# A fused Fourier mixing and squared-ReLU FFN on Trainium2: a third PSUM buffer out of the transform's banks, and more steps with P-Q+N on VectorE

## The chip, the cores and the metric

The kernel runs on one core of one Trainium2 chip. A core has five engines with a queue of instructions each, executed in order and tied together by semaphores: TensorE (PE; its weight loads are shown as PEld), VectorE (DVE), ScalarE (ACT), GpSimd (POOL) and SyncE (SP, which here only issues DMAs). Matmuls write to PSUM, which has 8 banks of 512 float32 columns in each of 128 partitions; VectorE and ScalarE read it. The metric is the device time of one execution in microseconds.

## The reference

```python
X = np.fft.fft(x, axis=1)              # x: 8 x 3008 x 256
X = np.fft.fft(X, axis=2)
t = X.real.reshape(8 * 3008, 256)
h = np.maximum(t @ w_in, 0.0)          # w_in: 256 x 2048
return h * h @ w_out                   # w_out: 2048 x 256
```

For each of 8 batches the real part of a two-dimensional Fourier transform is taken, and every one of the 24064 rows then goes through a feed-forward layer with 2048 hidden values, a ReLU and a square.

## The kernel before

**Pairs of tokens.** The second transform (over 256 values) is folded into `w_in` at the start: `gh[:, 0]` and `gh[:, 1]` are the cosine and the sine part of it times `w_in`, `gh[:, 2]` is the sine part times -2. With `zc` and `zs`, the cosine and sine parts of the first transform at a frequency k, the hidden values before the ReLU are P+Q for token k and P-Q (with a correction N for one row) for its mirror token S-k. So only half of the frequencies are computed: 12040 columns, in 25 windows or blocks (`wins`): 240, 512, 376, 376, 512, 448, then 512 each, and 360 in the last, block 24. Block w makes the hidden values of its columns and their mirrors.

**A block's steps.** A block has 8 steps (the loop at L1001), each for 256 of the 2048 hidden values (two chunks of 128). There are two kinds:

- A plain step: `pq` (L864) makes P+Q with four matmuls in a PSUM tile `ph` of two banks; ACT takes the ReLU out of it (`relu`, L893, with sign 0); `turn` (L888) adds -2Q with two more matmuls, which makes P-Q in the same tile; ACT takes that ReLU too (sign 1). DVE then squares the whole of both halves (`power`, L905).
- A step in `diff[w]`: `cosines` (L873) makes P alone with two matmuls; DVE makes t = -2P+N from it (`twice`, L879, from the rows `n` that POOL makes); `sines` (L883) adds Q with two matmuls; ACT takes the ReLU of P+Q and squares it (`power_act`, L909); DVE makes the ReLU of P-Q+N by a saturating add of t and `ph` (L898) and squares that half. Such a step has no `turn`.

`ph` has two buffers (`ps_h`, four banks). The saturating add of a step in `diff` is put off (`pend`) until behind the next step's `twice` if that step is in `diff` too. Where two such steps stand before a step, the next plain step begins with one piece of the second matmul of the FFN (L1024) ahead of `pq`. Squares are put off (`kept`) until the next step's `settle`. Between `pq` or `cosines` and `turn` or `sines`, `others` (L918) issues the rest of the step's work: the folds of the next batch (DVE, and transfers on POOL's queue), a part of the second matmul `po` (L713) of the block before, from its `h2`, and matmuls of the next window's transform. Most steps have 16 matmuls of `po`, of 256 columns; ACT copies `po` out to `osb` (L728), and SP's queue stores that.

**The transform's matmuls.** `z_steps` makes a unit (a batch's odd or even frequencies): four parts in the order zs/first, zc/first, zs/second, zc/second (`part` 1 is the sine part). Each part is an accumulation over 3 matmuls (odd) or 4 or 6 (even) in a PSUM tile `pz` of one bank, from a pool `ps_z` of two (L541). When a first part ends, ACT copies it to `es` (L548). The second parts go on in the tile that `st[part]` then names, a new one only where h and k are 0; ACT copies their sums into `zc` or `zs` (L554), and DVE makes the other half of the frequencies out of `es` and the same sums (`minus`, `apart`, L572). While `held["on"]` is set, which is where the next step is in `diff`, `minus` is kept back until `settle` has run in that step or until a new part begins (`let_go`). The matmuls of a unit are spread evenly over the steps from `lo` to `hi` of the block before the one that needs them.

**Order.** The order on every engine is the order of the program's text; there is no scheduler (`manual_schedule`). The framework follows tiles: it sets the semaphore waits between engines from the tiles that instructions read and write.

The last block's output (`tail`, L697) takes a PSUM tile for each group of 128 tokens, groups 2 and 3 of four from `ps_z` (L707).

Of the kernel before, what the change touches and what calls it, by code (L numbers as in the profile page):

```python
# [16 lines left out]
P = 128  # L17
R = 6
# [11 lines left out]
def kernel(  # L30
# [80 lines left out]
    drp = ctx.enter_context(tc.tile_pool(name="drp", bufs=2, space=bass.MemoryType.DRAM))  # L111
    ps_h = ctx.enter_context(tc.tile_pool(name="ps_h", bufs=2, space=bass.MemoryType.PSUM))
    ps_o = ctx.enter_context(tc.tile_pool(name="ps_o", bufs=2, space=bass.MemoryType.PSUM))
    ps_z = ctx.enter_context(tc.tile_pool(name="ps_z", bufs=2, space=bass.MemoryType.PSUM))

    XW = R * D

# [214 lines left out]
    def fold_steps(i):  # L332
# [42 lines left out]
        def v_part(sg):  # L375
# [6 lines left out]
                nc.vector.tensor_copy(ev[:, :, 0, 0:1], w[:, :, 0:1])  # L382
            nc.gpsimd.memset(ev[:, :, sg, 129:130], 0.0)

        def d_even(h=None):
            a, z = (0, 4 * R) if h is None else (2 * R * h, 2 * R * (h + 1))
            if a == 0:
                for o, v in ((t[0:1, 2, 0, :], t[0:1, 0, R - 1, :]), (fef[:, :, 0:1], xf[:, :, 0:1])):
                    if i > 1:
                        nc.scalar.activation(o, v, AF.Copy, bias=0.0, scale=1.0)  # L390
                    else:
                        nc.vector.tensor_copy(o, v)
            nc.vector.tensor_tensor(fef[:, a:z, 1:129], lo[:, a:z], hi[:, a:z], op=ALU.add)

        def d_odd(h=None):
# [72 lines left out]
            cp(spn[:, :, :, 0:1], rev_dim(yt[:, :, 0, :, 128:129], 1))  # L468

        late = [lambda: fold8(0), lambda: fold8(1), lambda: fold16(0), lambda: fold16(1), nyq8]  # L470
        return {"u_row": u_row, "edge": edge, "u_half": u_half, "u_odd": u_odd, "u_part": u_part, "v_even": v_even, "v_part": v_part, "d_even": d_even, "n_cos": n_cos, "odds": odds, "d_odd": d_odd, "load": load, "n_sin": n_sin, "nyq": nyq, "even": even, "away": away, "back": back, "late": late}

    gh = const.tile([P, 3, F], F16, name="gh")

# [47 lines left out]
    def z_steps(u, late=False):  # L522
# [15 lines left out]
        def mm(part, h, k, last, o0, o1, lhs, tab):  # L538
            if h == 0 and k == 0:
                let_go()  # L540
                st[part] = ps_z.tile([P, 512], F32, name="pz", tag="pz")  # L541
            ps = st[part]
            nc.tensor.matmul(ps[:, o0:o1], lhs, tab, start=(h == 0 and k == 0), stop=last, skip_group_check=True)  # L543
            if not last:
                return
            if h == 0:
                es = st["es", part] = evp.tile([P, NE], F32, name="es", tag="es")
                nc.scalar.activation(es[:, 0:n], ps[:, 0:n], AF.Copy, bias=0.0, scale=1.0)  # L548
                return
            es = st["es", part]  # L550
            for w, o, a, cnt in spans(c0, n):
                if late and w > 0:
                    continue
                nc.scalar.activation(zwin(w)[part][:, o : o + cnt], ps[:, a : a + cnt], AF.Copy, bias=0.0, scale=1.0)  # L554
            if not late:
                minus(part)
# [45 lines left out]
    def run(*jobs):  # L602
        for j in jobs:
            j()
# [91 lines left out]
    def ffn2_steps(w, h2, tail=False):  # L696
# [6 lines left out]
        def part(i, hf):  # L703
            q, m = groups[i]
            j = 0 if tail else i % 2
            if tail and hf == 0 and i % 4 > 1:
                st["po", i] = ps_z.tile([P, 512], F32, name="po", tag="pz")  # L707
            elif j == 0 and hf == 0:
                st["po", i] = ps_o.tile([P, 512], F32, name="po", tag="po")
            po = st["po", i - j]  # L710
# [40 lines left out]
    NST = NFC // 2  # L751
    at_of = {w: [[] for _ in range(NST)] for w in range(NW)}
    post_of = {w: [[] for _ in range(NST)] for w in range(NW)}
    diff = {w: (4, 6) if w < 6 else (1, 3, 5, 7) if w < NW - 4 else (1, 2, 4, 6, 7) for w in range(3, NW)}
    backs = []
    shared = []

    def put(w, s, i, name, *k, d=at_of):
        d[w][s].append(lambda: folds[i][name](*k))
# [1 line left out]
    def late(w, s, i, *st):  # L761
        at_of[w][s].append(lambda: run(*[folds[i]["late"][k] for k in st]))
# [4 lines left out]
    for i in range(2, B):  # L767
        b0 = (win_of(col_of[i, 0]) + win_of(col_of[i - 1, 1])) // 2 - 1
        tight = b0 - 2 in [(win_of(col_of[j, 0]) + win_of(col_of[j - 1, 1])) // 2 - 1 for j in range(2, i)]
        near = i == 2 or tight  # L770
        at_of[b0 - 1][0].append(lambda i=i: make(i))
        at_of[b0 - 2][7].append(lambda i=i: load_rows(i))
        backs.append(b0)
        late(b0 + 1, 3, i, 0)
        late(b0 + 1, 4, i, 1)
        for k in (2, 3, 4):
            late(b0 + 1, 5, i, k)
        put(b0 - 1, 5 if near else 3, i, "d_even", 0)
# [24 lines left out]
    plus = []  # L803
    pend = []

    def settle():
        for k in kept:
# [22 lines left out]
    for w in range(NW):  # L830
# [40 lines left out]
        t2s = {}  # L871

        def cosines(s):  # L873
            ph = phs[s] = ps_h.tile([P, 2, 512], F32, name="ph", tag="psh")
            for a in range(2):
                f0 = (2 * s + a) * P
                nc.tensor.matmul(ph[:, a, 0:wn], gh[:, 0, f0 : f0 + P], zcw[:, 0:wn], start=True, stop=True)  # L877
# [123 lines left out]
        for s in range(NST) if w > 1 else ():  # L1001
            held["on"] = s + 1 in diff.get(w, ())
            if s in diff.get(w, ()):
# [27 lines left out]
            nyq(s)  # L1031
            turn(s)
            relu(s, 1)
            if w in shared and s == 5:
                power_act(4, 1)
            keep(s, int(s == NST - 1), 2)
# [35 lines left out]
```

## Time and profile before

| | |
|---|---|
| median of 3 runs | 596.65 us (596.57 to 596.75) |
| the profiled execution | 596.79 us |
| its span, first to last instruction | 595.0 us |
| TensorE busy | 586.2 us (99%), 4430 matmuls |
| VectorE busy | 499.4 us (84%) |
| ScalarE busy | 463.0 us (78%) |
| GpSimd busy | 242.2 us (41%) |
| mean granted TensorE clock | 0.999 |

The views used are the page (busy times; 40 slices of the span; groups of instructions by line and form, with count, busy time, mean length of one, and the idle time of the engine ahead of them with what ended it), the sums of busy time in chosen windows, and the timeline (start, length, engine, line, operation and tiles, count of merged instructions). Times in the timeline count from the span's start. A row with a count of 2 or more runs from the first one's start to the last one's end; a matmul's row is longer than the distance to the next matmul, because matmuls overlap. The blocks begin at: 3 at 70.36, 6 at 133.60, 9 at 204.34, 10 at 229.72, 11 at 254.21, 21 at 492.86, 22 at 515.18, 23 at 538.71, 24 at 561.04; the last block's steps end at 580.4.

### The profile page before, as it was taken

The numbers are of one execution on the slowest core, as the hardware profiler recorded it, in microseconds if no ns is written. First come the engines' busy times: TensorE is split into PE (matmuls) and PEld (weight loads), VectorE is DVE, ScalarE is ACT, GpSimd is POOL, SyncE is SP. The second block draws the span as 40 slices with busy tenths as digits, with TensorE's granted clock in tenths as the row PEclk, the third lists the DMA queues.
The fourth block names the chain that finished last, engine by engine and source line by source line (L and its number), as shares of the span: only waits on it lengthen the run. The fifth ranks groups of instructions, "written<-read, shape, count | busy, mean of one in ns | idle before, by whom it ended". The sixth has DMA issues, their size and how long they took to land.

```text
span 595.0 us, 11318 instructions
## 1 busy us (share of the span) xinstructions
PE 586.2 (99%) x4430; PEld 426.0 (72%) x4430; DVE 499.4 (84%) x584; ACT 463.0 (78%) x620; POOL 242.2 (41%) x301
## 2 busy tenths in 40 slices
PE   9899999999999999999999999999999999999997
PEld 4567786776776777777777777777777777777786
DVE  8988686987889788978899899978899999889871
ACT  6796877967787787788878788877877788788762
POOL 8320423266504606182254651546505624425310
PEclk9999999999999999999999999999999999999999
DMA  8945421237211551246113442145312311211212
GB/s 150 170 86 135 124 72 44 54 102 150 58 47 52 134 133 53 73 99 151 42 58 113 94 115 55 38 121 117 88 39 90 89 56 37 61 47 48 61 56 70
DMA packets 37624, 50.33 MB, mean 85 GB/s; under 512 B 4589, under 2 KB 30755, under 8 KB 37571
## 3 DMA queue, kind: packets, MB, share of 16 engines
q0 software_dynamic: 10400, 24.94, 20.5%
q1 hardware_dynamic: 26899, 24.44, 13.6%
q8 instruction: 34, 0.56, 0.4%
q10 hardware_dynamic: 272, 0.23, 0.1%
q14 instruction: 19, 0.16, 0.1%
HBM read 36.42 MB, written 27.86 MB: 108 GB/s over the span
## 4 chain that ended last, share of the span: by engine, by line
PE 85%; DVE 7%; ACT 5%; issue 2%; ACTq 0%; DVEq 0%
PE po L713 48%; PE ph L891 7%; PE ph L868 7%; PE ph L869 7%; PE ph L886 6%; PE ph L877 5%; PE pz L543 4%; DVE h L907 2%; ACT h L900 2%; PE pw L310 2%; DVE t L881 2%; DVE h L898 2%; ACT h L911 1%; PE pg L489 1%; DVE zc L572 1%
## 5 line engine op out<-in xcount | busy, mean ns | idle before, releaser
L713 PE MATMUL po<-wout,h 128*128 128x256 f16 (+1 forms) x3024 | 364.8, 273 | 0.0
L713 PEld LDWEIGHTS <-h 128*128 128x128 f16 (+1 forms) x3024 | 296.9, 98 | 75.1
L900 ACT ACTIVATE h<-ph 128x1024 f16<-128x1024 f32 (+3 forms) x301 | 287.6, 991 | 64.2 <-PE ph L886 39.7
L907 DVE TENSOR_TENSOR h<-h 128x2048 f16<-128x2048 f16 (+7 forms) x199 | 193.2, 977 | 21.9 <-ACT h L900 16.9
L827 POOL TENSOR_SCALAR n<-zn,g2n 128x512 f32<-128x512 f16 (+3 forms) x166 | 155.6, 951 | 68.7 <-DMA zn<-rd 51.6
L881 DVE SCALAR_TENSOR_TENSOR t<-ph,n 128x1024 f32<-128x1024 f32 (+3 forms) x83 | 99.1, 1194 | 35.3 <-PE ph L877 31.7
L898 DVE CUSTOM_DVE_ANT_0 h<-t,ph 128x1024 f16<-128x1024 f32 x74 | 90.0, 1217 | 15.1 <-ACT h L900 13.8
L911 ACT ACTIVATE h<-h 128x1024 f16<-128x1024 f16 (+3 forms) x87 | 90.4, 1039 | 0.5
L728 ACT ACTIVATE osb<-po 128x512 f32<-128x512 f32 (+3 forms) x95 | 55.1, 585 | 37.0 <-PE po L713 32.5
L868 PE MATMUL ph<-zc,gh 128*128 128x512 f16 (+3 forms) x218 | 80.3, 369 | 0.4 <-ACT h L959 0.3
L869 PE MATMUL ph<-zs,gh 128*128 128x512 f16 (+3 forms) x218 | 80.2, 368 | 0.0
L819 POOL DMA_DIRECT2D zn<-rd x22 | 12.9, 585 | 161.4 <-DMA rd<-zs 146.3
L891 PE MATMUL ph<-zs,gh 128*128 128x512 f16 (+3 forms) x218 | 62.5, 368 | 0.4 <-ACT h L900 0.4
L886 PE MATMUL ph<-zs,gh 128*128 128x512 f16 (+3 forms) x166 | 48.4, 373 | 0.9 <-DVE t L881 0.4
L877 PE MATMUL ph<-zc,gh 128*128 128x512 f16 (+3 forms) x166 | 48.4, 373 | 0.0
L868 PEld LDWEIGHTS <-gh 128*128 128x128 f16 x218 | 21.2, 97 | 22.9 <-DVE h L898 1.6
L869 PEld LDWEIGHTS <-gh 128*128 128x128 f16 x218 | 21.3, 98 | 22.1 <-issue 0.9
L877 PEld LDWEIGHTS <-gh 128*128 128x128 f16 x166 | 16.2, 98 | 19.0 <-issue 0.5
L891 PEld LDWEIGHTS <-gh 128*128 128x128 f16 x218 | 20.2, 98 | 4.1 <-issue 0.7
L426 POOL DMA_DIRECT2D scr<-ev x8 | 4.7, 593 | 42.1 <-DVE ev L422 36.4
L548 ACT ACTIVATE es<-pz 128x376 f32<-128x376 f32 (+1 forms) x32 | 14.8, 485 | 8.9 <-PE pz L543 8.9
L436 POOL DMA_INDIRECT rb<-scr,idx_r x16 | 18.7, 1167 | 4.9 <-issue 4.9
(144 smaller groups left out, 368.6 us busy)
## 6 DMA issues: line engine op xcount, KB each, us to landing
out_dram<-osb SPq DMA_DIRECT2D x77, 128.0 KB
xo<-in_x_dram POOLq DMA_DIRECT2D x7, 768.0 KB
scr<-ev POOLq DMA_DIRECT2D x8, 390.0 KB
zn<-rd POOLq DMA_DIRECT2D x19, 128.0 KB
rb<-scr POOLq DMA_DIRECT2D x16, 130.0 KB
out_dram<-osb SPq DMA_DIRECT2D x12, 94.0 KB
w<-in_moe_w_in_dram POOLq DMA_DIRECT2D x2, 512.0 KB
wout<-in_moe_w_out_dram POOLq DMA_DIRECT2D x1, 1024.0 KB
```

The lines of the kernel that those rows point to most:

```text
L713: nc.tensor.matmul(po[0:m, j * D : (j + 1) * D], h2[:, fc, q : q + m], wout16[:, fc, :], start=(fc == 0 and not both), stop=(fc == NFC - 1 ...
L827: nc.gpsimd.tensor_scalar(out=n2[:, a, 0:wn1], in0=zns[wt][:, 0:wn1], scalar1=g2n[:, fc : fc + 1], scalar2=1.0, op0=ALU.mult, op1=ALU.mult)
L868: nc.tensor.matmul(ph[:, a, 0:wn], gh[:, 0, f0 : f0 + P], zcw[:, 0:wn], start=True, stop=False)
L869: nc.tensor.matmul(ph[:, a, 0:wn], gh[:, 1, f0 : f0 + P], zsw[:, 0:wn], start=False, stop=True)
L877: nc.tensor.matmul(ph[:, a, 0:wn], gh[:, 0, f0 : f0 + P], zcw[:, 0:wn], start=True, stop=True)
L881: nc.vector.scalar_tensor_tensor(out=t2[:, :, 0:wn], in0=phs[s][:, :, 0:wn], scalar=-2.0, in1=n2s[w, s][:, :, 0:wn], op0=ALU.mult, op1=ALU ...
L886: nc.tensor.matmul(phs[s][:, a, 0:wn], gh[:, 1, f0 : f0 + P], zsw[:, 0:wn], start=False, stop=True, skip_group_check=True)
L891: nc.tensor.matmul(phs[s][:, a, 0:wn], gh[:, 2, f0 : f0 + P], zsw[:, 0:wn], start=False, stop=True, skip_group_check=True)
L898: nc.vector._custom_dve(TENSOR_ADD_SAT, out=h, in0=t2s[s][:, :, 0:wn], in1=phs[s][:, :, 0:wn], s0=BIG, s1=0.0)
L900: nc.scalar.activation(h, phs[s][:, :, 0:wn], AF.Relu, bias=0.0, scale=-1.0)
L907: nc.vector.tensor_tensor(h, h, h, op=ALU.mult)
L911: nc.scalar.activation(h, h, AF.Square, bias=0.0, scale=1.0)
```

## The change

- The pool of two one-bank tiles for the transform becomes a single two-bank tile `zz`. A transform's new part takes its first or second bank in turn. The last block's output groups 2 and 3 of four take its banks too.
- In blocks 21, 23 and 24 (`threes`), the tiles `ph` go round three buffers: the two of `ps_h` and `zz`. Blocks 21 and 23 have no transform to make; block 22 has.
- `diff` changes: block 6 from (1, 3, 5, 7) to (1, 2, 4, 6, 7); block 9 from (1, 3) to (1, 2, 4); blocks 21 and 23 from (1, 2, 4, 6, 7) to (1, 2, 3, 5, 6, 7); block 24 from (1, 2, 4, 6, 7) to (1, 2, 3, 4, 5, 6, 7). That makes 89 such steps instead of 83.
- In blocks 21 and 23 the squares of the halves P-Q+N are put off to the next plain step (`aside`, on DVE) or given to ACT (`aside_act`, steps 3 and 7); in block 24 ACT squares those of steps 2 and 5. Block 6 joins the blocks in which ACT squares that half of step 4 (`shared`).
- In those three blocks the piece of the second matmul ahead of `pq` is left out.
- The two row copies at the head of `d_even` become a function `d_rows`, put one step earlier in block 9. The load of the input of transform 3 (`i + 1 = 3`) moves from block 5, step 7, to block 6, step 2.

```diff
-    ps_z = ctx.enter_context(tc.tile_pool(name="ps_z", bufs=2, space=bass.MemoryType.PSUM))
+    ps_z = ctx.enter_context(tc.tile_pool(name="ps_z", bufs=1, space=bass.MemoryType.PSUM))
+    zz = ps_z.tile([P, 2, 512], F32, name="zz")
+    turn_of = {"z": 0, "ph": 0}
...
+        def d_rows():
+            for o, v in ((t[0:1, 2, 0, :], t[0:1, 0, R - 1, :]), (fef[:, :, 0:1], xf[:, :, 0:1])):
...
-                st[part] = ps_z.tile([P, 512], F32, name="pz", tag="pz")
+                st[part] = zz[:, turn_of["z"] % 2, :]
+                turn_of["z"] += 1
...
-                st["po", i] = ps_z.tile([P, 512], F32, name="po", tag="pz")
+                st["po", i] = zz[:, i % 2, :]
...
-    diff = {w: (4, 6) if w < 6 else (1, 3, 5, 7) if w < NW - 4 else (1, 2, 4, 6, 7) for w in range(3, NW)}
+    diff = {w: (4, 6) if w < 6 else (1, 3, 5, 7) if 6 < w < NW - 4 else (1, 2, 4, 6, 7) for w in range(3, NW)}
+    diff[NW - 4] = diff[NW - 2] = (1, 2, 3, 5, 6, 7)
+    diff[NW - 1] = (1, 2, 3, 4, 5, 6, 7)
+    threes = (NW - 4, NW - 2, NW - 1)
+    by_act = (2, 5)
     backs = []
-    shared = []
+    shared = [6]
...
+        put(b0 - 1, 4 if tight else 5 if near else 3, i, "d_rows")
...
-        if i + 1 < B and b0 > 5 and (win_of(col_of[i + 1, 0]) + win_of(col_of[i, 1])) // 2 - 1 > b0 + 2:
+        if i + 1 < B and (win_of(col_of[i + 1, 0]) + win_of(col_of[i, 1])) // 2 - 1 > b0 + 2:
             put(b0 + 1, 2, i, "load")
...
         if tight:
-            diff[b0 - 1] = (1, 3)
+            diff[b0 - 1] = (1, 2, 4)
...
+        def bank():
+            if w in threes:
+                turn_of["ph"] += 1
+                if turn_of["ph"] % 3 == 0:
+                    return zz
+            return ps_h.tile([P, 2, 512], F32, name="ph", tag="psh")
+
         def pq(s):
-            ph = phs[s] = ps_h.tile([P, 2, 512], F32, name="ph", tag="psh")
+            ph = phs[s] = bank()
...
-                whole = w in shared and s == 4
+                whole = w in shared and s == 4 or w in threes[:2] or w == NW - 1 and s in by_act
                 pend.append(lambda s=s, r=relu, k=keep, whole=whole: (r(s, 1), whole or k(s, 1, 2)))
+                if w in threes[:2] and s % 4 < 3:
+                    aside.append(lambda s=s, p=power: p(s, 1, 2))
...
+                act_squares()
+                if w in threes[:2] and s % 4 == 3 or w == NW - 1 and s in by_act:
+                    aside_act.append(lambda s=s, p=power_act: p(s, 1))
...
-            if made[s] and made[s + 1]:
+            if made[s] and made[s + 1] and w not in threes:
                 f2s[s].pop(0)()
             pq(s)
+            kept.extend(aside)
+            aside.clear()
             settle()
```

More of the change, by code (lines that the diff above doesn't have):

```diff
@@ L383, in v_part @@
             nc.gpsimd.memset(ev[:, :, sg, 129:130], 0.0)
+        def d_rows():
+            for o, v in ((t[0:1, 2, 0, :], t[0:1, 0, R - 1, :]), (fef[:, :, 0:1], xf[:, :, 0:1])):
+                if i > 1:
+                    nc.scalar.activation(o, v, AF.Copy, bias=0.0, scale=1.0)
+                else:
+                    nc.vector.tensor_copy(o, v)
         def d_even(h=None):
             a, z = (0, 4 * R) if h is None else (2 * R * h, 2 * R * (h + 1))
[L387 to L392, printed above, removed]
+            if h is None:
+                d_rows()
             nc.vector.tensor_tensor(fef[:, a:z, 1:129], lo[:, a:z], hi[:, a:z], op=ALU.add)
@@ L470, in fold_steps @@
         late = [lambda: fold8(0), lambda: fold8(1), lambda: fold16(0), lambda: fold16(1), nyq8]
-        return {"u_row": u_row, "edge": edge, "u_half": u_half, "u_odd": u_odd, "u_part": u_part, "v_even": v_even, "v_part": v_part, "d_even": d_even, "n_cos": n_cos, "odds": odds, "d_odd": d_odd, "load": load, "n_sin": n_sin, "nyq": nyq, "even": even, "away": away, "back": back, "late": late}
+        return {"u_row": u_row, "edge": edge, "u_half": u_half, "u_odd": u_odd, "u_part": u_part, "v_even": v_even, "v_part": v_part, "d_rows": d_rows, "d_even": d_even, "n_cos": n_cos, "odds": odds, "d_odd": d_odd, "load": load, "n_sin": n_sin, "nyq": nyq, "even": even, "away": away, "back": back, "late": late}
     gh = const.tile([P, 3, F], F16, name="gh")
@@ L804, with act_squares @@
     pend = []
+    aside = []
+    aside_act = []
+    def act_squares():
+        run(*aside_act)
+        aside_act.clear()
     def settle():
@@ L873, in cosines @@
         def cosines(s):
-            ph = phs[s] = ps_h.tile([P, 2, 512], F32, name="ph", tag="psh")
+            ph = phs[s] = bank()
             for a in range(2):
@@ L1033 @@
             relu(s, 1)
+            act_squares()
             if w in shared and s == 5:
```

## The prediction

> **What bounds the kernel now.** I read the page's busy times and slices first, then the sums of single blocks, then the groups by form.
>
> ```profile
> PE 586.2 (99%) x4430; PEld 426.0 (72%) x4430; DVE 499.4 (84%) x584; ACT 463.0 (78%) x620; POOL 242.2 (41%) x301
> PEclk9999999999999999999999999999999999999999
> ```
>
> ```profile
> 133.60:156.87 23.27, 23.11 (x165) 16.02 (x164) 19.68 (x25) 17.92 (x24) 13.10 (x16) 1.00 0.57 123
> 204.34:229.72 25.38, 25.38 (x186) 18.00 (x185) 19.19 (x26) 19.88 (x28) 6.76 (x9) 1.00 0.51 110
> 229.72:254.21 24.49, 24.40 (x193) 17.91 (x192) 21.97 (x24) 18.68 (x27) 11.24 (x12) 1.00 0.24 72
> 492.86:515.18 22.32, 22.32 (x167) 16.08 (x167) 19.38 (x19) 17.73 (x21) 6.19 (x8) 1.00 0.19 50
> 538.71:561.04 22.33, 22.33 (x168) 16.10 (x167) 19.76 (x19) 17.73 (x21) 11.60 (x16) 1.00 0.18 54
> 561.04:580.40 19.36, 19.36 (x164) 15.90 (x164) 15.00 (x19) 13.69 (x20) 4.12 (x6) 1.00 0.20 55
> ```
>
> These are blocks 6, 9, 10, 21, 23 and 24 (length; then PE, PEld, DVE, ACT, POOL busy; granted clock): TensorE is busy without a break at a granted clock of 1.00. So it sets the end, a matmul left out is worth its whole length, and each time TensorE is held is added whole.
>
> **What is removed.** Six more steps leave out the two matmuls of `turn`: one each in blocks 6, 9, 21, 23 (512 columns), two in block 24 (360). The start of such a pair, and of what follows it:
>
> ```profile
> 543.51 0.59 PE L886 MATMUL ph<-zs,gh 128*128 128x512 f16 x2
> 543.94 0.59 PE L877 MATMUL ph<-zc,gh 128*128 128x512 f16 x2
> 580.08 0.47 PE L886 MATMUL ph<-zs,gh 128*128 128x360 f16 x2
> 580.38 10.64 PE L713 MATMUL po<-wout,h 128*128 128x256 f16 x96
> ```
>
> A pair takes 0.43 us, or 0.30: 4 x 0.43 + 2 x 0.30 = **2.3 us less**.
>
> **What is added elsewhere.**
>
> ```profile
> L907 DVE TENSOR_TENSOR h<-h 128x2048 f16<-128x2048 f16 x78 | 97.5, 1253 | 7.7 <-ACT h L900 7.2
> L881 DVE SCALAR_TENSOR_TENSOR t<-ph,n 128x1024 f32<-128x1024 f32 x74 | 90.5, 1223 | 30.8 <-PE ph L877 28.5 <-POOL n L827 0.6 <-POOL spn L468 0.6
> L898 DVE CUSTOM_DVE_ANT_0 h<-t,ph 128x1024 f16<-128x1024 f32 x74 | 90.0, 1217 | 15.1 <-ACT h L900 13.8 <-issue 1.0
> L907 DVE TENSOR_TENSOR h<-h 128x1024 f16<-128x1024 f16 x86 | 67.5, 791 | 5.0 <-ACT h L900 1.9 <-issue 0.7
> L911 ACT ACTIVATE h<-h 128x1024 f16<-128x1024 f16 x78 | 82.7, 1061 | 0.4
> ```
>
> After the change block 21 has on DVE 6 x (1.22 + 1.22) + 4 half squares x 0.79 + 2 whole x 1.25 = 20.3 us, against 22.32 - 0.43 = 21.9 us of TensorE. ACT gives up one minus relu and takes one square more of each kind: 17.73 + 3 x 1.06 - 1.0 = 19.9 us. Both still fit, and with a third PSUM buffer the next cosines need not wait for the saturating add of two steps before, so I count the runs at nothing; their cover is 1.6 us a block on DVE, and without it up to one 1.22 us add is exposed per run. Blocks 6 and 9 get one such step each: DVE +1.22 +1.22 +0.79 -1.25 = +2.0 us on 19.7 of 23.3 and 19.2 of 25.4, no fuller than block 10 with 22.0 of 24.5, in which TensorE does not wait: nothing. POOL makes 12 more rows of `n` in time that it idles (6.19 of 22.32 us busy in block 21). `d_rows` moves two short copies on ACT up to a step earlier in block 9; the load of transform 3 moves from step 5.7 to 6.2, past four pairs of `n` rows on POOL, still nine steps ahead of its first reader. Both are hidden: zero, or a few tenths if the data are late.
>
> **What the third buffer costs: the transform's two banks become one tile.** Before, each part of a transform took its own one-bank tile from a pool of two. Now both are slices of one tile `zz`. The list of the built program's instructions on TensorE, with the semaphores each waits for, shows what follows. Block 10, step 1, after:
>
> ```
> 3420 L549 Matmult zz<-cos_659,spn 128x95
> 3421 L549 Ldweights xy
> 3422 L549 Matmult zz<-cos_659,xy 128x188 [waits Activation_49]
> ```
>
> and before:
>
> ```
> 3428 L543 Matmult pz<-cos_662,spn 128x95
> 3429 L543 Ldweights xy
> 3430 L543 Matmult pz<-cos_662,xy 128x188
> ```
>
> The first matmul of a part now waits until ACT has copied out the part before it, though that lies in the other bank; 47 transform matmuls wait where 19 did, and some for DVE's `minus` too. Where a part ends inside a step, nothing stands between the two matmuls and TensorE stands still. What is queued behind is everything: the rest of the transform, `turn` or `sines`, the next block step.
>
> One such wait stands in the old trace (block 1, the same bank used again):
>
> ```profile
> 43.40 4.09 DVE L907 TENSOR_TENSOR h<-h 128x2048 f16<-128x2048 f16 x4
> 44.05 0.64 PE L543 MATMUL pz<-cos,od 128*128 128x376 f16 x3
> 44.25 0.96 ACT L548 ACTIVATE es<-pz 128x376 f32<-128x376 f32 x2
> 44.79 0.64 PE L543 MATMUL pz<-sin,od 128*128 128x376 f16 x3
> 45.26 0.64 PE L543 MATMUL pz<-cos,od 128*128 128x376 f16 x3
> 47.41 0.54 DVE L572 SCALAR_TENSOR_TENSOR zs<-es,pz 128x376 f16<-128x376 f32 x1
> ```
>
> The first copy ends at 44.73 and TensorE starts at 44.79: it resumes 0.06 us after the copy. So a hold is: end of the copy in the old trace + 0.06 - old start of the next part. In block 1 the last part now waits for DVE's `minus`, which stands behind four squares: 47.41 + 0.54 + 0.06 - 45.26 = **2.75** (the two holds ahead of it fall into the same time).
>
> ```profile
> 81.39 0.24 PE L543 MATMUL pz<-cos,xy 128*128 128x188 f16 x1
> 81.59 0.86 ACT L548 ACTIVATE es<-pz 128x377 f32<-128x377 f32 x2 [0.87 <-PE pz L543]
> 86.19 0.25 PE L543 MATMUL pz<-cos,xy 128*128 128x188 f16 x1
> 86.91 0.62 DVE L572 SCALAR_TENSOR_TENSOR zs<-es,pz 128x135 f16<-128x135 f32 x2
> ```
>
> Block 3: ACT is free; the first of two copies ends at 82.08, 0.75; then one behind `minus`, 87.53 + 0.06 - 86.19 = 1.40. **2.15.**
>
> ```profile
> 104.76 0.24 PE L543 MATMUL pz<-sin,xy 128*128 128x188 f16 x1
> 106.37 0.48 ACT L548 ACTIVATE es<-pz 128x377 f32<-128x377 f32 x1
> 107.27 0.24 PE L543 MATMUL pz<-cos,xy 128*128 128x188 f16 x1
> 108.94 0.60 DVE L572 SCALAR_TENSOR_TENSOR zs<-es,pz 128x342 f16<-128x342 f32 x2
> ```
>
> Block 4: the copy stands behind a square, two row copies and an output copy, 2.15; then 109.54 + 0.06 - 107.27 = 2.33 at most, 0.75 at least; I take 2.0, near the upper end, since DVE has a whole square ahead. **4.15.**
>
> ```profile
> 235.70 0.24 PE L543 MATMUL pz<-cos,xy 128*128 128x188 f16 x1
> 235.86 0.60 ACT L728 ACTIVATE osb<-po 128x512 f32<-128x512 f32 x1 [0.67 <-PE pz L543]
> 236.35 0.86 ACT L548 ACTIVATE es<-pz 128x377 f32<-128x377 f32 x2
> 241.94 0.25 PE L543 MATMUL pz<-cos,xy 128*128 128x188 f16 x1
> 242.74 0.56 ACT L554 ACTIVATE zs<-pz 128x269 f16<-128x269 f32 x2
> 526.54 0.25 PE L543 MATMUL pz<-cos,xy 128*128 128x188 f16 x1
> 527.74 0.49 ACT L554 ACTIVATE zs<-pz 128x377 f16<-128x377 f32 x1
> ```
>
> Block 10: an output copy stands ahead; 236.83 + 0.06 - 235.70 = 1.19, and 243.30 + 0.06 - 241.94 = 1.42, so 2.6; blocks 13, 16, 19 are built alike: **10.4**. Block 22, the last: 1.19 + (528.23 + 0.06 - 526.54 = 1.75) = **2.9**.
>
> Without rows of their own, by those just seen: blocks 7 and 9 have two holds each between 0.75 and 1.19, at 1.0: **4.0**; block 9 also one behind `minus`, because step 4 becomes a `twice` step, and the `minus` made at the end of step 3 is kept back until behind its `twice` and a whole square (1.22 + 1.25): 0 to block 4's 2.3, taken as block 3's **1.4**, in the middle; the start two free ones, at most 0.75 each, the second partly over while the first runs: **1.3**; the last block's output, where group 3 waits for group 2's copy: **0.65**. In blocks 6, 11, 14, 17, 20 a part ends with its step, 2.1 us or more of other matmuls lie between, and nothing is held.
>
> Sum: 2.75 + 2.15 + 4.15 + 10.4 + 2.9 + 4.0 + 1.4 + 1.3 + 0.65 = 29.7; less 2.3: **+27.4**. The profiled execution took 596.79 us, 595.0 of it span and 1.8 around it, 0.14 above the median 596.65. 596.8 + 27.4 = 624.2; I say **624**.
>
> [...] The old trace agrees that the banks are independent: TensorE writes at 81.39 while ACT reads the other bank at 81.59. But the program's list has the waits, so the sum goes by the list.
>
> **Rivals.** *The halves stay independent in effect*: 596.8 - 2.3 = **594.5**, faster. It needs the holds to come to under 2.3 us together, below 0.1 us each. For it: the old rows show the overlap. Against it: 44.79 shows such a wait holding TensorE to the end of the copy. 0.04.
> *The long runs bind on DVE as well*: 20.3 of 21.9 us leaves little for an order that doesn't fit; one add of 1.22 us exposed in each of four runs of three and twice in block 24 makes 7 more, **631**. Against it: three PSUM buffers, and ACT takes part of the squares. 0.07.
> *The holds slow TensorE's clock.*
>
> ```profile
> 1.22 10.75 PE L310 MATMUL pw<-spn 128*128 128x384 f16 x48 [1.22 <-DVE spn L189]
> 12.29 2.44 PE L310 MATMUL pw<-spn 128*128 128x384 f16 x14
> ```
>
> After the idle start 48 of these took 10.75 us, where at the later rate (2.44 / 14 = 0.174) they take 8.4: a fall costs about 2.4 us. Blocks 1 and 4 have the long holds: two falls, **629**. [...] 0.03.
>
> **How the numbers follow.** Forecast 0.85, the three rivals 0.14, other 0.01. Low end: holds behind `minus` cost the copy alone (-4) and later holds of the old kernel are absorbed (-3): 617, taken as 616. High end: the second rival, 631, and the weights' loads behind some waits: 632. Faster 0.04, within 0.2% (1.2 us, about what a measurement can tell) 0.01, slower 0.95.
>
> **What would show it.** In the chain and groups, idle time of TensorE before L549, ended by ACT `es`, `zs` and DVE `zs`, of 25 to 30 us in some 25 places; blocks 10, 13, 16 and 19 longer by 2.6 us each; blocks 11, 14, 17 and 20 unchanged; blocks 21, 23, 24 shorter by 0.43, 0.43 and 0.6 us. No idle time before L549 would prove me wrong; a block 21 or 23 longer than 22.3 us would speak for the second rival.

## The result and the profile after

The changed kernel takes 623.71 us (median of 5 runs, 622.37 to 623.89) beside 596.75 us (596.57 to 596.87) for the kernel before on the same chip: a ratio of 1.0445, 95% interval 1.0433 to 1.0457, so 27 us slower. The profiled execution took 623.89 us, 622.0 of it span.

The page after has TensorE at 95% where it had 99%, and for the first time a digit below 9 in the row of its clock:

```profile
PE 587.8 (95%) x4418; PEld 426.0 (68%) x4418; DVE 499.4 (80%) x589; ACT 473.0 (76%) x627; POOL 247.7 (40%) x313
PEclk9998999999999999999999999999999999999999
```

The view of waits (engine, tile and line; who ended the wait; us in total, times, longest) has at its head three rows that the kernel before does not have at all. L549 is the transform's matmul, L554 and L560 are ACT's two kinds of copies out of the transform's tile, and L578 is DVE's `minus`:

```profile
PE zz L549 <- ACT es L554: 12.6, 14, 2.0
PE zz L549 <- ACT zs L560: 6.5, 5, 1.6
PE zz L549 <- DVE zs L578: 5.5, 4, 1.6
```

These are 24.6 us in 23 waits. Taken from matmul to matmul, the gaps in the TensorE stream at these places and in the last block's output are 25 and come to 29.7 us, because each gap is a little longer than what the view puts down to its releaser; two of them stood in the kernel before as well, with 0.26 us each, so 29.2 us are new. One of the 25, block 10, step 1, in the timeline:

```profile
251.14 0.21 PE L549 MATMUL zz<-cos,spn 128*128 128x95 f16 x1
251.34 0.60 ACT L734 ACTIVATE osb<-po 128x512 f32<-128x512 f32 x1 [0.67 <-PE zz L549]
251.84 0.48 ACT L554 ACTIVATE es<-zz 128x377 f32<-128x377 f32 x1
252.37 0.24 PE L549 MATMUL zz<-cos,xy 128*128 128x188 f16 x1 [1.02 <-ACT es L554]
```

The part whose last matmul starts at 251.14 is copied out only after an output copy, until 252.32. The next part, which writes the other bank, starts at 252.37, 0.05 us after the copy's end.

The sums by block (span; busy times of PE, PEld, DVE, ACT, POOL with counts; granted clock, DMA share, GB/s), here of blocks 1, 10, 11 and 21:

```profile
29.34:54.22 24.88, 22.08 (x143) 13.78 (x143) 18.12 (x22) 18.54 (x23) 3.20 (x3) 0.93 0.52 97
...
245.20:272.05 26.85, 24.59 (x193) 17.98 (x192) 21.94 (x24) 18.95 (x27) 11.06 (x12) 1.00 0.22 65
272.05:296.63 24.58, 24.58 (x184) 17.71 (x182) 20.02 (x26) 20.10 (x29) 12.75 (x17) 1.00 0.58 129
...
518.29:540.53 22.24, 22.24 (x168) 16.37 (x168) 19.50 (x18) 19.14 (x22) 8.37 (x11) 1.00 0.20 51
```

Block 10 is 2.36 us longer than before, block 11, where each part of the transform ends with its step, is unchanged, and block 21 is only 0.08 us shorter. From the first matmul of each block in the traces, the lengths of all blocks against those before, and the same for three of the experiments below (all in us; "kernel before" is the length, the other columns are differences to it):

```
block            kernel before   changed   one tile alone   tiles apart   whole parts
start                28.29        +1.05        +1.06           -0.20         +1.07
1                    20.46        +4.42        +4.41            0.00         +4.08
3                    18.66        +2.13        +2.14            0.00         +1.36
4                    22.23        +3.12        +3.11            0.00         +3.19
5, 6                 45.62        +0.33        +1.47           +0.05         +0.06
7                    24.33        +1.52        +1.95           -0.43         -0.29
9                    25.38        +2.91        +1.79           -0.43         +1.04
10                   24.49        +2.36        +2.36           +0.13         -0.23
13, 16               49.00        +4.70        +4.69            0.00         -0.48
14                   24.57        +0.17        +0.01           +0.36          0.00
19                   24.49        +2.72        +2.36            0.00         +0.18
21                   22.32        -0.08        +0.01           -0.08         -0.08
22                   23.53        +2.30        +2.79           -0.50         -0.61
23                   22.33        -0.59         0.00           -0.58         -0.58
24 and output        29.98        +0.45        +0.63           -0.18         +0.45
```

The last row runs to the end of the last matmul. The blocks that are not listed differ by 0.01 at most. A piece of four matmuls (0.43 us) at a border is counted on the other side of it after the change: it leaves block 7 for 6, and blocks 20, 22 and 23 for the block behind each.

**The clock.** Block 1 has more than its holds. Its last hold and what follows, in the timeline (L932 are the squares ahead of `minus`):

```profile
44.45 4.09 DVE L932 TENSOR_TENSOR h<-h 128x2048 f16<-128x2048 f16 x4
...
47.83 0.48 ACT L560 ACTIVATE zs<-zz 128x376 f16<-128x376 f32 x1 [0.73 <-PE zz L549]
48.46 0.54 DVE L578 SCALAR_TENSOR_TENSOR zs<-es,zz 128x376 f16<-128x376 f32 x1
49.05 0.78 PE L549 MATMUL zz<-cos,od 128*128 128x376 f16 x3 [1.26 <-DVE zs L578]
...
50.48 1.06 PE L916 MATMUL ph<-zs,gh 128*128 128x512 f16 x2
```

The pair of `turn` at 50.48 shows 1.06 us where such a pair has 0.59. Three stretches, each as long (3.41 us) as the fall that the second of them shows; block 1's holds of 0.80 and 1.42 us lie in the first:

```profile
46.00:49.41 3.41, 1.52 (x9) 0.71 (x8) 3.00 (x4) 0.97 (x2) 0.00 (x0) 1.00 1.09 214
49.41:52.82 3.41, 3.41 (x14) 2.34 (x13) 0.55 (x1) 1.51 (x2) 0.00 (x0) 0.50 0.19 37
52.82:56.24 3.42, 3.42 (x42) 2.90 (x41) 1.85 (x4) 2.36 (x4) 0.00 (x0) 1.00 0.21 66
```

After a stretch in which TensorE was busy for 1.52 of 3.41 us, the granted clock was 0.50 for 3.41 us and then 1.00 again. Of the five executions three have a mean clock of 0.997 and took 623.71 to 623.89 us, two have 1.000 and took 622.37 and 622.57. So a fall costs about 1.3 us (623.73 - 622.47, the medians of the two groups), and it happens in some executions only.

### The profile page after: what moved, and what is told of

Read it like the earlier page. It is cut to its first block, busy times and chain, and to the rows that moved or that the text cites. A ratio compares the mean times of both kernels' runs of the same rounds, so it can differ in the third digit from the quotient of the medians.

```text
span 622.0 us, 11338 instructions
## 1 busy us (share of the span) xinstructions
PE 587.8 (95%) x4418; PEld 426.0 (68%) x4418; DVE 499.4 (80%) x589; ACT 473.0 (76%) x627; POOL 247.7 (40%) x313
## 3 DMA queue, kind: packets, MB, share of 16 engines
q0 software_dynamic: 10400, 24.94, 19.9%
## 4 chain that ended last, share of the span: by engine, by line
PE 82%; DVE 8%; ACT 6%; issue 2%; DMA 1%; SPq 0%; POOL 0%; ACTq 0%; DVEq 0%; POOLq 0%
PE po L719 46%; PE ph L916 7%; PE ph L893 6%; PE ph L894 6%; PE ph L911 5%; PE ph L902 5%; PE zz L549 4%; DVE t L906 2%; ACT h L925 2%; DVE h L932 2%; ACT h L936 1%; ACT osb L734 1%; DVE h L923 1%; ACT es L554 1%; PE zz L719 1%
## 5 line engine op out<-in xcount | busy, mean ns | idle before, releaser
L925 ACT ACTIVATE h<-ph 128x1024 f16<-128x1024 f32 (+3 forms) x286 | 273.6, 991 | 68.0 <-PE ph L911 39.6
L932 DVE TENSOR_TENSOR h<-h 128x1024 f16<-128x1024 f16 (+6 forms) x192 | 180.7, 949 | 20.7 <-ACT h L925 17.4
L936 ACT ACTIVATE h<-h 128x1024 f16<-128x1024 f16 (+3 forms) x100 | 102.7, 1029 | 0.8
L923 DVE CUSTOM_DVE_ANT_0 h<-t,ph 128x1024 f16<-128x1024 f32 x74 | 90.0, 1216 | 15.9 <-ACT h L925 15.3
L893 PE MATMUL ph<-zc,gh 128*128 128x512 f16 (+2 forms) x204 | 75.3, 369 | 0.6 <-DVE h L923 0.3
L894 PE MATMUL ph<-zs,gh 128*128 128x512 f16 (+2 forms) x204 | 75.2, 369 | 0.0
L916 PE MATMUL ph<-zs,gh 128*128 128x512 f16 (+2 forms) x204 | 59.4, 373 | 0.2
L911 PE MATMUL ph<-zs,gh 128*128 128x512 f16 (+3 forms) x164 | 47.9, 373 | 0.6 <-DVE t L906 0.4
L902 PE MATMUL ph<-zc,gh 128*128 128x512 f16 (+3 forms) x164 | 47.9, 374 | 0.0
L893 PEld LDWEIGHTS <-gh 128*128 128x128 f16 x206 | 20.1, 97 | 22.2 <-DVE h L923 1.6
L894 PEld LDWEIGHTS <-gh 128*128 128x128 f16 x206 | 20.1, 98 | 20.8 <-issue 0.5
L902 PEld LDWEIGHTS <-gh 128*128 128x128 f16 x178 | 17.4, 98 | 19.8
L549 PE MATMUL zz<-cos,xy 128*128 128x188 f16 (+1 forms) x64 | 10.6, 225 | 16.0 <-ACT es L554 6.7
L549 PEld LDWEIGHTS <-xy 128*128 128x128 f16 x128 | 11.2, 97 | 21.1 <-issue 17.3
L554 ACT ACTIVATE es<-zz 128x376 f32<-128x376 f32 (+1 forms) x32 | 15.4, 482 | 13.0 <-PE zz L549 13.0
```

Source lines behind the costliest of these rows:

```text
L911: nc.tensor.matmul(phs[s][:, a, 0:wn], gh[:, 1, f0 : f0 + P], zsw[:, 0:wn], start=False, stop=True, skip_group_check=True)
L916: nc.tensor.matmul(phs[s][:, a, 0:wn], gh[:, 2, f0 : f0 + P], zsw[:, 0:wn], start=False, stop=True, skip_group_check=True)
L923: nc.vector._custom_dve(TENSOR_ADD_SAT, out=h, in0=t2s[s][:, :, 0:wn], in1=phs[s][:, :, 0:wn], s0=BIG, s1=0.0)
L925: nc.scalar.activation(h, phs[s][:, :, 0:wn], AF.Relu, bias=0.0, scale=-1.0)
L932: nc.vector.tensor_tensor(h, h, h, op=ALU.mult)
L936: nc.scalar.activation(h, h, AF.Square, bias=0.0, scale=1.0)
```

## The experiments

**One tile alone.** My theory is that the change of tile by itself makes the loss. The rival is that it comes from the longer runs of steps. The kernel before, with nothing changed but this:

```diff
-    ps_z = ctx.enter_context(tc.tile_pool(name="ps_z", bufs=2, space=bass.MemoryType.PSUM))
+    ps_z = ctx.enter_context(tc.tile_pool(name="ps_z", bufs=1, space=bass.MemoryType.PSUM))
+    zz = ps_z.tile([P, 2, 512], F32, name="zz")
...
-                st[part] = ps_z.tile([P, 512], F32, name="pz", tag="pz")
+                st[part] = zz[:, turn_of["z"] % 2, :]
+                turn_of["z"] += 1
...
-                st["po", i] = ps_z.tile([P, 512], F32, name="po", tag="pz")
+                st["po", i] = zz[:, i % 2, :]
```

> The kernel before, with one edit: the transform's two one-bank tiles become the two banks of one tile. No step more leaves out its `turn`, no third buffer. Theory (each hand-over of the tile holds TensorE until the copy of the other bank has ended): the holds measured in the changed kernel come to 29.2 us; block 9's third one, 1.54 there, needs the new step 4 of that block and stays out or shrinks to a plain copy (0.7), and up to 1.7 us more where the clock falls in block 1. So 596.75 + 28 = 625, range 623.5 to 627. Rival (the longer runs of steps or the moved work cost the time): no change, 596.7.

It took 625.19 us (623.59 to 625.48), 1.0471 times the kernel before (1.0455 to 1.0487). Its waits (L546, L551, L557 and L575 are the lines of the transform's matmul, the two copies and `minus` there) are those of the changed kernel:

```profile
PE zz L546 <- ACT es L551: 12.6, 14, 2.0
PE zz L546 <- ACT zs L557: 6.5, 5, 1.6
PE zz L546 <- DVE zs L575: 5.4, 4, 1.6
```

So the tile alone makes the loss; the rest of the change takes 1.5 us off again. The column of block lengths shows where the two kernels differ: block 9 lacks the hold of 1.54 that comes with its new step 4, as expected; block 6 has one of 1.46 that the changed kernel does not have, since there the steps (1, 3, 5, 7) put a `twice` in front of the last part's `minus`. I had not seen that one.

**The tiles apart.** The changed kernel, with the transform's own one-bank tiles back and the third buffer kept:

```diff
-                st[part] = zz[:, turn_of["z"] % 2, :]
-                turn_of["z"] += 1
+                st[part] = zpool["pool"].tile([P, 512], F32, name="pz", tag="pz")
...
-                st["po", i] = zz[:, i % 2, :]
+                st["po", i] = zpool["pool"].tile([P, 512], F32, name="po", tag="pz")
...
+        z_open(w in threes)
```

`z_open` closes the pool of two one-bank tiles at the start of blocks 21, 23 and 24, opens in its two banks a pool with the tile of two banks, and puts the first pool back at the start of block 22 and before the output.

> The changed kernel with one edit: the transform keeps its two one-bank tiles, and the two-bank tile exists only in blocks 21, 23 and 24, where no transform is running. Theory: all holds before the transform and the fall of the clock go, and what is left is the gain of the six matmul pairs, 2.3 us, less the 0.49 us by which block 21 starts late: 596.75 - 2.3 + 0.5 = 594.9, range 594.2 to 595.6. Rival (the runs of three and seven steps cost on VectorE too): 597 or more.

It took 594.97 us (594.86 to 595.47), 0.9972 of the kernel before (0.9962 to 0.9982). The page has TensorE at 98% and its clock at 9 throughout, and none of the three waits is left in the view of waits:

```profile
PE 583.1 (98%) x4418; PEld 424.6 (72%) x4418; DVE 500.6 (84%) x589; ACT 470.9 (79%) x627; POOL 248.5 (42%) x313
PEclk9999999999999999999999999999999999999999
```

The same place in block 10, in its timeline:

```profile
234.65 0.21 PE L560 MATMUL pz<-cos,spn 128*128 128x95 f16 x1
234.69 0.24 PE L560 MATMUL pz<-cos,xy 128*128 128x188 f16 x1
234.85 0.60 ACT L745 ACTIVATE osb<-po 128x512 f32<-128x512 f32 x1 [0.67 <-PE pz L560]
235.35 0.86 ACT L565 ACTIVATE es<-pz 128x377 f32<-128x377 f32 x2
```

The next part starts 0.04 us after the one before it, 0.66 us before the copy of the first even begins. In the built programs of both kernels `ps_h` and `ps_o` hold the banks 0 to 5, and `zz` and the one-bank tiles lie in the banks 6 and 7, so the two banks are the same ones, and the copies are as long (0.48 us for one there, 0.86 for two here); only the tiles differ. So the wait is the program's, set by the framework per tile: in this run two banks needed no wait for each other, and in the changed kernel they had one, of 1.18 us from matmul to matmul at this place, because they were one tile.

With the holds gone, the gain of the left-out pairs can be seen: 596.71 - 594.97 = 1.74 us of the 2.3 forecast. At block 21 nearly nothing is saved (the next experiment), and blocks 10 and 14, whose steps did not change, have new waits behind `twice` and the add that make them 0.13 and 0.36 longer. In block 14 VectorE starts a `twice` 0.37 us later than in the kernel before; why stays open. With the wait of 0.49 in block 21 that is 1.0 us not saved; against it, the start is 0.20 shorter, and blocks 22 to 24 together are 0.23 shorter than their pairs explain.

**The piece ahead in block 21.** The changed kernel starts block 21 with `pq` at once. Its timeline there (L923 is the saturating add, L911 the sines of block 20's last step, L893 the first matmuls of block 21):

```profile
517.02 1.21 DVE L923 CUSTOM_DVE_ANT_0 h<-t,ph 128x1024 f16<-128x1024 f32 x1
517.37 0.59 PE L911 MATMUL ph<-zs,gh 128*128 128x512 f16 x2
518.29 0.39 PE L893 MATMUL ph<-zc,gh 128*128 128x512 f16 x1 [0.33 <-DVE h L923]
```

Both buffers are the old ones there, because the third comes only in turn. The add frees one at 518.23, and TensorE has nothing else to do: 0.49 us from matmul to matmul. The edit, on the kernel with the tiles apart:

```diff
-            if made[s] and made[s + 1] and w not in threes:
+            if made[s] and made[s + 1] and (w not in threes or (w, s) == (NW - 4, 0)):
```

> As the kernel with the tiles apart, but block 21 puts one piece of the output product ahead of its first pair, as the kernel before did. Theory: the 0.49 us in which TensorE waits there for VectorE's add of the block before goes: 594.4, and block 21 is 0.4 us shorter than in the kernel before. Rival (the wait is only put off to step 1, because one buffer is still held): 594.9, no gain.

594.59 us (594.43 to 594.92), 0.9965 of the kernel before (0.9952 to 0.9979), and block 21 takes 21.80 us:

```profile
492.46:514.26 21.80, 21.80 (x166) 15.96 (x165) 19.49 (x18) 19.03 (x22) 8.53 (x11) 1.00 0.20 52
```

The piece is now counted in block 20, which takes 24.58 us as before: it is done in the time of the wait. Block 21 is 0.44 shorter than without the piece ahead and 0.52 shorter than in the kernel before. The medians differ by 0.38, and the ranges overlap by 0.06. With the wait gone from the trace at that place, I take the term as shown: dropping the piece cost what the missing pair saved.

**Two buffers instead of three.** The kernel with the tiles apart, where `bank()` never returns the third buffer (`if w in threes:` becomes `if w in ():`). This measures what the buffer is for.

> As the kernel with the tiles apart, but blocks 21, 23 and 24 use only the two old buffers for their pairs; the runs of three and seven steps stay. Theory: from the third step of a run on, the cosines find both buffers held until VectorE's add of two steps before, as at the start of block 21, where TensorE waits 0.49 us. That is 4 steps in blocks 21 and 23, 5 in block 24 and 3 pairs that follow a run: 12 x 0.49 = 5.9, so 600.9, range 598 to 606 (12 whole adds of 1.22 would be 14.6). Rival (the third buffer brings nothing, two are enough): 595.

599.02 us (598.98 to 599.63), 1.0041 times the kernel before (1.0028 to 1.0054): 4.05 us slower than with three. In its waits the cosines (L914) and `pq` (L905) now wait for the add (L935):

```profile
PE ph L905 <- DVE h L935: 1.6, 5, 0.3
PE ph L914 <- DVE h L935: 1.3, 4, 0.3
```

From matmul to matmul each of the nine is 0.49 to 0.50 us, the price seen in block 21; eight of them are new, 8 x 0.49 = 3.9. My sum had twelve: I had counted five inside block 24's run of seven, and not the pair at the head of block 23, which follows steps 6 and 7 of block 22. In the run of seven the instructions are for 360 columns, and the add ends just as TensorE gets there:

```profile
576.95 0.89 DVE L935 CUSTOM_DVE_ANT_1 h<-t,ph 128x720 f16<-128x720 f32 x1
577.57 0.47 PE L923 MATMUL ph<-zs,gh 128*128 128x360 f16 x2
577.90 0.48 PE L914 MATMUL ph<-zc,gh 128*128 128x360 f16 x2
```

So runs of three without the third buffer would have cost more than they save. The third buffer does its work; its banks were taken in the wrong way.

**Whole parts.** The prediction said that a hand-over costs only where nothing lies between two parts. The changed kernel, one tile and all, with whole parts spread over the steps in place of single matmuls:

```diff
-                zl[:] = [j for zu, part, h in zj for j in zu(part, h)]
+                zl[:] = [lambda js=zu(part, h): run(*js) for zu, part, h in zj]
```

> The changed kernel, one two-bank tile and all, but each part of the transform is issued whole in a step of its own (4 or 6 matmuls a step in place of 5 and 5), so that some two us of other matmuls lie between two parts. Theory (a hand-over costs only where nothing lies between): the holds in blocks 3, 7, 9, 10, 13, 16, 19 and 22 go, and one of block 4's two; by the holds measured that is 2.1 + 2.0 + 1.95 + 3.3 + 10.3 + 2.9 = 22.6 us, less up to 1.5 where the copy is late even so: 601 to 602.5. The start and block 1 stay as they are. Rival (each hand-over costs wherever it stands): 623 to 624.

605.60 us (604.37 to 605.87), 1.0144 times the kernel before (1.0129 to 1.0160): 18.1 us of the 22.6 came back. In blocks 10, 13, 16 and 22 not only do the holds go, they get shorter than in the kernel before. My number, 601 to 602.5, missed because of three blocks. The waits that stay (the three behind `es` are in the start and in block 1):

```profile
PE zz L549 <- DVE zs L578: 5.9, 4, 2.2
PE zz L549 <- ACT es L554: 1.8, 3, 0.6
```

And block 4's in the timeline (L932 is the square):

```profile
114.18 1.22 DVE L932 TENSOR_TENSOR h<-h 128x2048 f16<-128x2048 f16 x1 [0.26 <-ACT h L925]
115.32 0.60 DVE L578 SCALAR_TENSOR_TENSOR zs<-es,zz 128x342 f16<-128x342 f32 x2
115.98 0.26 PE L549 MATMUL zz<-cos,xy 128*128 128x188 f16 x1 [2.17 <-DVE zs L578]
```

Where the next part waits for `minus` and not for a copy, some two us of other matmuls are not enough, because `minus` stands behind a whole square or is kept back behind `twice`: 1.34 us stay in block 3 and 1.46 in block 9, and in block 4 a hold of 2.33 takes the place of two of 2.15 and 1.76. Behind that hold, which ends at 115.98, the clock falls a second time in this execution (stretches of 3.41 us):

```profile
113.29:116.70 3.41, 1.24 (x15) 0.84 (x14) 2.38 (x4) 1.56 (x5) 0.00 (x0) 1.00 0.25 77
116.70:120.11 3.41, 3.41 (x14) 2.35 (x13) 2.75 (x5) 2.73 (x5) 0.00 (x0) 0.50 0.00 0
```

**The single tile from block 2 on.** This prices the start and block 1, holds and clock together. The changed kernel with a pool of two one-bank tiles at first, and from block 2 on the one tile in the same banks:

```diff
-                st[part] = zz[:, turn_of["z"] % 2, :]
-                turn_of["z"] += 1
+                if zpool["on"]:
+                    st[part] = zpool["pool"].tile([P, 512], F32, name="pz", tag="pz")
+                else:
+                    st[part] = zpool["zz"][:, turn_of["z"] % 2, :]
+                    turn_of["z"] += 1
...
+        if w == 2:
+            z_join()
```

> The changed kernel, but the transform has its two one-bank tiles in the start and in block 1, and the one two-bank tile from block 2 on. Theory: the start is 1.05 us shorter and block 1 as long as in the kernel before, 4.4 us shorter, holds (2.75) and slowed clock (1.66) together: 623.7 - 5.45 = 618.3, range 617.6 to 619, and no run shows a fall of the clock. Rival (the clock falls somewhere else instead, in block 4, where the holds are as long): 620.

618.59 us (618.34 to 620.15), 1.0378 times the kernel before (1.0364 to 1.0392). The start and block 1 are as long as in the kernel before (28.08 and 20.47 us), every other block as in the changed kernel. But my second clause was wrong: of the five executions three have a clock of 0.999 or more and took 618.34 to 618.59, and two have 0.997 and took 620.07 and 620.15. So a fall also comes without block 1's holds, as the rival had it, and costs 1.6 us here. The profiled execution is one of the three without it, so where the fall of the other two lies is not shown; block 4, where whole parts had a fall, is my guess.

**`minus` ahead of the squares in block 1.** The prediction put block 1's last hold down to the four squares that stand before `minus` on DVE.

```diff
+                    run(*zl)
                     settle()
                     power(s1, 0, 1)
-                    run(*zl)
```

> The changed kernel, but in block 1 VectorE makes the `minus` of the transform ahead of the four squares that stood before it. TensorE's order is the same. Theory (the last hold is only the queue on VectorE, and the clock falls when TensorE works too little over some 3.4 us, 0.35 of the time in the profile of the changed kernel, while 0.40 in block 4 brought no fall): the last hold falls from 1.42 to about 0.8 and the clock stays: 622.0, range 621.5 to 622.6, no run with a fall. Rival (three holds in a row are enough for a fall): 623.1, with falls in most runs.

622.12 us (621.99 to 623.96), 1.0439 times the kernel before (1.0425 to 1.0454). The time is as I expected, the reason is not. In its timeline DVE is idle and the hold is still there, 1.32 us in place of 1.42:

```profile
47.18 0.64 PE L549 MATMUL zz<-sin,od 128*128 128x376 f16 x3 [0.63 <-ACT es L554]
47.86 0.48 ACT L560 ACTIVATE zs<-zz 128x376 f16<-128x376 f32 x1 [0.73 <-PE zz L549]
48.37 0.55 DVE L578 SCALAR_TENSOR_TENSOR zs<-es,zz 128x376 f16<-128x376 f32 x1 [3.79 <-ACT zs L560]
48.97 0.64 PE L549 MATMUL zz<-cos,od 128*128 128x376 f16 x3 [1.15 <-DVE zs L578]
```

`minus` starts 0.03 us after ACT's copy of the same part has ended: the two run one after the other, 0.48 + 0.55 us, and then the next part starts. The squares end at 44.45 + 4.09 = 48.54 in the changed kernel's profile, that is, at nearly the same moment, so that either would have made the hold.

The clock did not settle the second question as I had put it. Three executions have a clock of 1.000 (621.99 to 622.12) and two have 0.997 (623.75 and 623.96). The profiled one is without a fall, with these two stretches over the holds:

```profile
44.06:47.48 3.42, 1.88 (x12) 0.89 (x10) 0.18 (x1) 2.28 (x4) 0.00 (x0) 1.00 1.08 212
47.48:50.89 3.41, 2.26 (x17) 1.58 (x15) 1.27 (x3) 1.34 (x3) 0.00 (x0) 1.00 0.76 149
```

Both are at a granted clock of 1.00, with 1.88 and 2.26 us of matmuls. Why two executions of this kernel have a fall and three have none is not shown, and that the work in some 3.4 us decides it was my estimate, which no run here shows.

**All that paid, together.** The tiles apart, the piece ahead in block 21, and whole parts in blocks 10, 13, 16, 19 and 22:

```diff
                 zl[:] = [j for zu, part, h in zj for j in zu(part, h)]
+                if len(zl) == 20 and hi - lo == 4 and w > 9:
+                    zl[:] = [lambda js=zu(part, h): run(*js) for zu, part, h in zj]
```

> As the kernel with the tiles apart and the piece ahead in block 21, and in blocks 10, 13, 16, 19 and 22 each part of the transform issued whole in a step of its own (6, 4, 6 and 4 matmuls in place of 5 each). Theory: the small waits of 0.1 to 0.4 us that stand later in these blocks and in block 14 go, as they did with whole parts on the single tile: -0.36 -0.24 -0.24 -0.11 -0.36 +0.18 = -1.1, so 593.5, range 593.0 to 594.2. Rival (they went there because the blocks were longer before): 594.6.

593.44 us (593.25 to 593.82), 0.9945 of the kernel before (0.9932 to 0.9959): 3.2 us faster than the kernel before and 30.3 us faster than the changed one. Blocks 10, 13, 16 and 14 are shorter by 0.36, 0.23, 0.23 and 0.36 us than with the tiles apart alone, block 22 by 0.1, and block 19 is 0.17 longer. Block 10 for one:

```profile
228.87:253.13 24.26, 24.26 (x193) 17.82 (x192) 21.15 (x24) 18.74 (x27) 11.25 (x12) 1.00 0.23 70
```

The sum of its parts, 1.1 us, came. Why a step of whole parts avoids these small waits of 0.1 to 0.4 us later in the block stays open.

## Why the prediction was right, and where it was off

The forecast was 624 us in a range from 616 to 632, and the measured time is 623.71. The mechanism is the one it named, and the wait is where it said: one tile alone makes the loss, the tiles apart take it away. The terms, forecast against measured:

- *The holds.* As gaps in the TensorE stream: 29.7 forecast, 29.2 measured beyond those of before. Blocks 10, 13, 16 and 19: 2.6 forecast each, 1.18 + 1.40 = 2.58 measured. Block 3: 2.15 and 2.13. Block 22: 2.9 and 2.91. Output: 0.65 and 0.64. Start: 1.3 and 1.27. Block 4: 4.15 and 3.91. Blocks 7 and 9: 5.4 and 1.95 + 3.34 = 5.29. In the time, without a fall of the clock, they count for less: 622.47 - 596.75 = 25.7, and 1.74 for the pairs, make 27.5. The step that was too high is the one that added each hold whole: where waits already stood in the same block they shrank or went (in block 4 three waits, 0.97 us in all from matmul to matmul, became one of 0.22, and the block is only 3.12 longer; 0.22 each went in blocks 10, 13 and 16). The prediction had put that into the low end, at up to 3 us, and not into the sum.
- *Block 1.* 2.75 forecast, 0.78 + 0.80 + 1.42 - 0.26 = 2.74 measured. The number came out, the stated cause did not: without the four squares the last hold is only 0.1 us shorter. It is set by copy (0.48 us), then `minus` (0.55), then matmul, one after the other.
- *Less work in `turn`.* 2.3 forecast, 1.74 with the tiles apart. The step that failed took the pairs' whole length as saved and did not price the piece that is no longer ahead of `pq` in blocks 21, 23 and 24: in block 21 its absence exposed 0.49 us. In blocks 23 and 24 it cost nothing. The new waits in blocks 10 and 14, 0.49 together, were not in the sum either, and small gains elsewhere made up for part of both.
- *Blocks 6 and 9 at nothing.* Right: with the tiles apart, blocks 5 to 7 are 0.38 shorter and block 9 is 0.43 shorter, where a pair takes 0.43. The reading given for it was not: block 10 was said to have no wait of TensorE, but its row in the profile before has 24.40 of 24.49 us busy, and at 250.74 there is a gap of 0.26 from matmul to matmul, behind a `twice`.
- *Runs of three and seven at nothing.* Right: blocks 23 and 24 save what their pairs take, or a little more. Their cover is the third buffer, without which eight more places cost 0.49 each, not the 1.22 of a whole add that the prediction named. So the rival in which long runs bind on DVE is out, with 19.5 of 22.24 us busy in block 21 where the prediction had 20.3 of 21.9. ACT has 19.1 us there, not 19.9: the block has one instruction of ACT more than before (22 for 21), and the sum had counted two more.
- *The independent halves* (594.5) is the time of the kernel with the tiles apart (594.97), which shows the price of that rival right and its condition not met: it needed two tiles.
- *The clock.* This rival came true beside the forecast, at 1.3 us in 3 of 5 executions, not the 4.8 that the prediction put on two falls. The prediction gave it 0.03, on my estimate of how long a hold would have to be, which no run shows; that is the step that failed: the profiled execution has a fall at 49.41, behind holds of 0.78, 0.80 and 1.42 us in block 1, and none behind those of 2.15 and 1.76 us in block 4. The price of 2.4 us a fall was an estimate too, from the matmuls of the start, where the view of the kernel before gives the clock as 1.00 (0 to 14 us). Without a fall the changed kernel takes 622.4 to 622.6. So the sum was some 1.7 us high, 2.2 for the holds less 0.6 for the pairs, and the fall, at 1.3, brought the median back to it: the forecast is closer than its terms, and that much closer by luck.
- *The signs.* Idle time before the transform's matmuls (24.6 us in 23 waits by the view) and blocks 11, 17 and 20 are as said. Block 14 is 0.17 longer where it was to be unchanged, block 21 only 0.08 shorter where it was to be 0.43, and block 24 with the output 0.45 longer, since the hold of 0.64 and the piece of 0.43 fall into it.

## What to carry to other kernels

The framework here sets waits per tile, and so made two banks wait for each other once they were slices of one tile: that alone took the kernel before from 596.71 to 625.19 us. Before two buffers are joined into one to lend them elsewhere, list who writes the one half while the other is read; or open the joined tile only for the stretch that borrows it, which here turned 27 us lost into 1.7 won, and 3.2 with the piece ahead and the whole parts.

On an engine that is the bound, price a hand-over as the wait for the last reader's end, with everything that is queued ahead of that reader (29.7 us forecast so, 29.2 measured); some two us of other work between two parts hid every copy in the kernel with whole parts (the three waits behind `es` that stay, 1.8 us in all, are in the start and block 1), and did not hide a reader that was itself queued behind a square (2.33 us in block 4).

## What the runs showed of the hardware that was not expected

The clock of TensorE fell to 0.50 for 3.41 us in block 1 of the changed kernel, where the 3.41 us ahead have 1.52 us of matmuls and a longest gap of 1.42, and in block 4 of the kernel with whole parts, where they have 1.24 and a longest gap of 2.33. There was no fall behind the two stretches with 1.88 and 2.26 in block 1 of the kernel with `minus` ahead, and none behind this one in block 4 of the changed kernel:

```profile
110.85:114.26 3.41, 1.54 (x16) 1.31 (x15) 2.80 (x3) 3.38 (x7) 0.00 (x0) 1.00 0.00 0
114.26:117.68 3.42, 2.67 (x22) 1.96 (x21) 1.96 (x2) 1.64 (x4) 0.00 (x0) 1.00 0.25 77
```

But one fall, in block 1 of the kernel with whole parts, came behind a stretch with as much work as the first of these:

```profile
45.02:48.43 3.41, 1.54 (x8) 0.62 (x7) 3.41 (x4) 1.80 (x4) 0.00 (x0) 1.00 1.07 209
48.43:51.85 3.42, 2.79 (x10) 1.72 (x10) 1.13 (x3) 0.48 (x1) 0.00 (x0) 0.50 0.45 89
```

So the busy time in such a stretch does not tell the two apart: 1.54 stands on both sides. It also hangs on where the stretch is begun: from 111.50 to 114.91 of the changed kernel it is 1.42, less than the 1.52 ahead of its fall, and the clock stays at 1.00. What brings a fall is not shown. One fall cost 1.3 to 1.8 us, by the medians of the executions with and without it in four kernels (the changed one 1.3, the joined tile from block 2 on 1.6, `minus` ahead 1.7, one tile alone 1.8).
